# Linear attention and a gated feed-forward on one core: the second tile's loads ahead of the output weights, its attention inside the first tile's units, the first tile's outputs inside the second tile

## The chip, the cores and the metric

The kernel runs on one core of a Trainium2 chip. The metric is device time in microseconds, the median of the runs. One more execution was taken with the hardware profiler; every row shown comes from it. The engines are TensorE (PE in the profile; PEld is its weight load), VectorE (DVE), ScalarE (ACT), GpSimd (POOL) and SyncE (SP). Each works through its own instructions in the order in which they were issued, and waits at the first whose inputs or whose output buffer are not free.

## The reference

Decayed linear attention over 4 batches, 8 heads, 768 positions and 64 channels, in blocks, and then a gated feed-forward on the 3072 positions of width 512, with an inner width of 1536.

```python
for b in range(nb):                                # blocks of 64 positions
    intra = np.einsum('bhic,bhjc->bhij', qb, kb) * Dmask[None]
    intra = np.einsum('bhij,bhjd->bhid', intra, vb)
    inter = np.einsum('bhid,bhde->bhie', qb * lam_pow[None], kv_state)
    out[:, :, sl] = intra + inter
    kv_state = lam_block * kv_state + np.einsum('bhsd,bhse->bhde', kb * rev_pow[None], vb)
x = attn_out.transpose(0, 2, 1, 3).reshape(B * S, H * D)
g = x @ w_gate
out = (g * (1.0 / (1.0 + np.exp(-g))) * (x @ w_val)) @ w_out
```

## The kernel before, in words

The 768 positions are cut into six tiles (`NBLK`) of 128 positions; a tile holds all 4 batches, so 512 rows. For each tile the attention of the four batches gives `xt` (the feed-forward's input, transposed), then twelve `ffn_fc` units give the hidden rows, then four `ffn_out` give the output rows of the four batches.

The order is written by hand. Each tile has a list of units, and `pieces` says which parts of the attention are issued behind which unit: dictionaries `late` (tile 0), `second` (tile 1) and the result of `spread` (later tiles). The instructions of every engine stand in exactly this order.

A unit `ffn_fc` (L369) is four matmuls for `gp`, Silu on ScalarE, four matmuls for `vp`, and a product `h_sb` on VectorE. `gp` and `vp` take turns in three PSUM buffers (`gpsum`). An output `ffn_out` (L384) is twelve matmuls, a copy on ScalarE and a store from SP.

The attention of one batch of one tile has these parts. `prep_k` (L206) transposes K with eight matmuls, and ScalarE copies the result to `ktb` in two halves. `prep_q` (L214) transposes Q with four matmuls, and VectorE scales it into `qt`. `front` (L247) makes the scores, which VectorE masks into `ssb`; in tiles 0 and 1 it fills two score buffers, in later tiles one. `values` (L271) applies the scores to V and the state to Q; the result is copied to `xt`. `scale_v` (L298) makes the product `v_s` of V and the decay, in two halves of 64 partitions: on VectorE for tiles 0 and 1, on GpSimd from tile 2 on (`HALF`). `update` (L314) multiplies K by that product and brings the running state `kv` and its decayed form `kvd` up to date on VectorE; `cast_kv` copies the state to `kvb` on ScalarE. From tile 2 on, `update_mid` (L334), `cast_mid` and `update_end` do this in two steps of 64 positions. All PSUM tiles of the attention and of the outputs share three buffers (`apsum`), the scores have two (`spsum`).

In tile 2 (Q only) and from tile 3 on (`TURNED`; K and Q) the transposes are done by DMA instead, issued from SP (`turn`, L230).

Loads of K, Q, V and of the weights are issued from GpSimd, and they cast to bf16 on the way. They use eight semaphores in turn, so a load waits until the one eight before it has landed. K and V have three slots in SBUF; each needs its off-diagonal parts zeroed once, which GpSimd does with memsets for the slots 1 and 2. GpSimd issues, after the eight loads of the gate and value weights:

```python
nc.gpsimd.dma_start(out=wo_sb, in_=moe_w_out.rearrange("(c p) m -> p c m", p=128))
nc.gpsimd.memset(kvb[:, 0].bitcast(U32), 0)
zero_off(nc.gpsimd, ktb[:, 1])
for slot in (1, 2):
    for t in (kbd, vbd):
        zero_off(nc.gpsimd, t[:, slot])
load_k(1); load_qv(1, 2)
load_k(2); load_qv(2)
```

Tile 0 has the twelve units and then its own outputs (three whole, the last in two halves of the columns). The whole attention of tile 1 stands between these outputs. Tile 1 has only its twelve units, with the attention of tile 2 and the last two updates of tile 1 in between. From tile 2 on, the outputs of the tile before stand behind every third unit. The last tile's outputs end the kernel.

Of the kernel before, what the change touches and what calls it, by code (L numbers as in the profile page):

```python
# [21 lines left out]
def kernel(  # L22
# [73 lines left out]
    def load_k(tt):
        for c in range(2):
            load_bd(k, kbd, tt, c)

    def load_qv(tt, step=B, between=()):  # L100
        qn[tt] = load.tile([128, B, H, D], BF16, name="q_nat", tag="q_nat")
        for b in range(0, B, step):
            load_q(tt, b, b + step)
            for f, *on in between:
                f(*on)
            for c in range(2):
                load_bd(v, vbd, tt, c, b, b + step)
# [84 lines left out]
    wo_sb = const.tile([128, FC, DM], BF16, name="wo_sb")  # L192
# [13 lines left out]
    def prep_k(tt, b, pool=apsum, tag="a"):  # L206
        tk = pool.tile([128, 2, HP, 64], FP32, name="tk", tag=tag)
        for hp in range(HP):
            for c in range(2):
                nc.tensor.matmul(tk[:, c, hp, :], kbd[:, tt % SLOTS, c, b * HP + hp, :], eye2, start=True, stop=True)  # L210
        for h, ps in enumerate(HALVES):
            nc.scalar.copy(out=ktb[ps, tt % 2, :, b * HP:(b + 1) * HP, 64 * h:64 * h + 64], in_=tk[ps])  # L212
# [84 lines left out]

    def scale_v(tt, b):  # L298

        v_s = att.tile([128, HP, 2, D], BF16, name="v_s", tag="v_h" if tt >= HALF else "v_s")  # L300
        for h, ps in enumerate(HALVES):
            vb = vbd[ps, tt % SLOTS, 0, b * HP, 64 * h:64 * h + 64]
            eng = nc.gpsimd if tt >= HALF else nc.vector
            n = 1 if tt == NBLK - 1 else 2
            pv = bap(pw[ps], [[7, HP], [0, n], [0, D]], extra_offset=3) if tt >= HALF else \
                bap(pw[ps], [[7, HP], [1, n], [0, D]], extra_offset=2)
            eng.tensor_tensor(out=v_s[ps, :, 0:n], in0=bap(vb, [[128, HP], [128 * NP, n], [1, D]]), in1=pv,  # L307
                              op=ALU.mult)
        scaled[tt, b] = v_s
# [88 lines left out]
    for b in range(2):  # L398
        prep_q(0, b)
# [23 lines left out]
    load_qv(2)

    late = {1: []}
    for b in range(B):
        late.setdefault(3 * b, []).append((scale_v, 0, b))
        late[3 * b + 2] = [(update, 0, b)]  # L430
        late[3 * b + 3] = [(cast_kv, b)]
    late[1].append((zero_mid,))
    late[13] = [(prep, 1, 0, gpsum, "g"), (prep, 1, 1, gpsum, "g"), (scale_v, 1, 0)]
    late[14] = [(front, 1, 0), (front, 1, 1), (prep, 1, 2, gpsum, "g"), (prep, 1, 3, gpsum, "g"),
                (scale_v, 1, 1), (values, 1, 0)]
    late[15] = [(values, 1, 1), (front, 1, 2), (front, 1, 3), (update, 1, 0), (values, 1, 2),
                (update, 1, 1), (values, 1, 3), (cast_kv, 0), (cast_kv, 1)]

    def spread(tt, at, slots):

        for b, (s0, s1, s2, s3, s4) in enumerate(slots):
            for i, f, *on in ((s0, scale_q if tt >= TURNED else prep_k, tt, b), (s1, update_mid, tt, b),
                              (s2, cast_mid, b), (s2, front, tt, b), (s2, update_end, tt, b), (s3, values, tt, b),
                              (s4, cast_kv, b)):
                if f is not cast_kv or tt + 1 < NBLK:
                    at.setdefault(i, []).append((f, *on))
                if f is prep_k:
                    at[i].append((scale_q, tt, b))
        return at


    late[14].append((turn, 2, 2))
    late[15].append((scale_v, 1, 2))
    second = {0: [(update, 1, 2), (scale_v, 1, 3)], 1: [(cast_kv, 2)], 2: [(update, 1, 3)], 3: [(cast_kv, 3)]}
    second = spread(2, second, ((1, 2, 3, 4, 5), (3, 4, 5, 6, 7), (6, 7, 8, 9, 10), (7, 8, 9, 10, 11)))

    for tt in range(NBLK):
        units = [(ffn_fc, tt, fc) for fc in range(FC)]
        pieces = {}
        if tt == 0:  # L460
            units += [(ffn_out, 0, b) for b in range(3)] + [(ffn_out, 0, 3, i, 2) for i in range(2)]
            pieces = late
        else:
            if tt + 1 < NBLK:
                for b in range(2):
                    scale_v(tt + 1, b)
            rest = [(scale_v, tt + 1, b) for b in range(2, B)] if tt + 1 < NBLK else []
            if tt + 2 < NBLK:
                load_k(tt + 2)
                load_qv(tt + 2, between=rest)  # L470
            else:
                for f, *on in rest:
                    f(*on)
            if tt > 1:
                units = sum([units[3 * b:3 * b + 3] + [(ffn_out, tt - 1, b)] for b in range(B)], [])
            if tt == 1:
                pieces = second
            elif tt + 1 < NBLK:
                pieces = spread(tt + 1, {}, [(max(i - 1, 0), i, i + 1, i + 2, i + 3) for i in (0, 4, 8, 12)])
# [41 lines left out]
```

## Time and profile before

| | us |
|---|---|
| median of 3 runs (237.81 to 238.08) | 238.0 |
| the profiled execution | 239.77 |
| its span, first to last instruction | 238.0 |
| TensorE busy | 219.2 |
| VectorE busy | 122.7 |
| ScalarE busy | 123.4 |
| GpSimd busy | 102.5 |

The granted clock of TensorE is 1.00 throughout. The profiled execution's time contains 1.8 us around its span. These points in time help to read the timelines (us from the start of the span): first unit of tile 0 at 19.09; first output of tile 0 at 40.77; first unit of tile 1 at 59.04; first unit of tile 2 at 87.11; last matmul issued at about 234.

The loads, with the time from issue to landing: the last piece of the value weights issued at 17.20 lands 14.5 us later; the output weights issued at 17.93 land 21.5 us later; tile 1's K is issued from 29.74 and lands after 10.4 to 10.6 us; its last V is issued at 45.3 and lands after 4.8 us.

### The profile page before, as it was taken

What the parts mean: (1) busy time and instruction counts of PE and PEld (TensorE: products, weight loads), DVE (VectorE), ACT (ScalarE), POOL (GpSimd) and SP (SyncE); (2) the same over time, 40 slices, a digit from 0 to 9 for tenths busy, and PEclk for the clock granted to TensorE, in tenths of its full rate; (3) what the DMA queues carried; (4) which work ended last, traced back from release to release, by engine and by line L of the source; (5) the groups of instructions that cost most, each with busy time, mean ns of one, the idle gap of its engine ahead of it and who ended that gap; (6) DMA issues with size and microseconds to landing.
All of it is one profiled execution on the core that took longest, in us unless ns stands there. A gap on an engine that the chain in (4) does not pass through costs nothing.

```text
span 238.0 us, 4373 instructions
## 1 busy us (share of the span) xinstructions
PE 219.2 (92%) x1692; PEld 118.2 (50%) x1720; DVE 122.7 (52%) x233; ACT 123.4 (52%) x234; POOL 102.5 (43%) x125
## 2 busy tenths in 40 slices
PE   0598999988989997999999999999999999999994
PEld 0484454567455544455545545555455544444443
DVE  7685677288798677356457247336334412322100
ACT  7875644466758883546545545554534532232122
POOL 7999992891699319971997302200000000000000
PEclk9999999999999999999999999999999999999999
DMA  7999999999989994999999895100110110111022
GB/s 110 194 176 201 206 207 170 178 179 168 165 57 134 129 171 59 113 215 174 168 131 141 132 116 130 47 31 13 47 44 0 47 44 2 42 47 44 35 101 88
DMA packets 105269, 26.50 MB, mean 111 GB/s; under 512 B 96288, under 2 KB 102432, under 8 KB 105248
## 3 DMA queue, kind: packets, MB, share of 16 engines
q0 software_dynamic: 76400, 13.64, 74.9%
q1 hardware_dynamic: 28704, 12.59, 24.2%
q8 instruction: 13, 0.21, 0.3%
q14 instruction: 8, 0.07, 0.1%
q10 hardware_dynamic: 144, 0.00, 0.0%
HBM read 28.32 MB, written 6.29 MB: 145 GB/s over the span
## 4 chain that ended last, share of the span: by engine, by line
PE 60%; POOL 21%; DMA 15%; issue 2%; ACT 0%; POOLq 0%; ACTq 0%
PE ffn_op L391 22%; PE vp L381 17%; PE gp L376 17%; DMA vbd<-in_v_dram 10%; POOL kbd L86 5%; DMA q_nat<-in_q_dram 5%; POOL v_s L307 4%; POOL vbd L86 2%; POOL q_nat L92 1%; PE op L279 1%; PE sp L254 1%; PE op L280 1%; PE up L340 1%; POOL wv_sb L195 1%; POOL wg_sb L195 1%
## 5 line engine op out<-in xcount | busy, mean ns | idle before, releaser
L382 DVE TENSOR_TENSOR h_sb<-sil,vp 128x512 bf16<-128x512 bf16 x72 | 49.4, 686 | 85.5 <-PE vp L381 51.8
L381 PE MATMUL vp<-xt,wv_sb 128*128 128x512 bf16 x281 | 73.4, 379 | 0.5
L376 PE MATMUL gp<-xt,wg_sb 128*128 128x512 bf16 x274 | 72.0, 379 | 1.2 <-ACT xt L291 0.5
L378 ACT ACTIVATE sil<-gp 128x512 bf16<-128x512 f32 x72 | 43.0, 597 | 44.9 <-PE gp L376 40.8
L391 PE MATMUL ffn_op<-wo_sb,h_sb 128*128 128x512 bf16 (+1 forms) x305 | 64.3, 362 | 0.3
L307 POOL TENSOR_TENSOR v_s<-vbd,pw 64x512 bf16<-64x512 bf16 (+1 forms) x32 | 30.9, 966 | 43.5 <-DMA vbd<-in_v_dram 24.2
L381 PEld LDWEIGHTS <-wv_sb 128*128 128x128 bf16 x288 | 28.2, 98 | 34.0
L391 PEld LDWEIGHTS <-h_sb 128*128 128x128 bf16 x312 | 29.5, 98 | 28.6
L394 ACT COPY osb<-ffn_op 128x512 f32<-128x512 f32 (+1 forms) x26 | 14.4, 553 | 48.1 <-PE ffn_op L391 46.9
L376 PEld LDWEIGHTS <-wg_sb 128*128 128x128 bf16 x288 | 25.6, 98 | 25.4 <-issue 0.7
L86 POOL DMA_DIRECT2D vbd<-in_v_dram x32 | 24.3, 787 | 5.1 <-DMA wo_sb<-in_moe_w_out_dram 4.2
L86 POOL DMA_DIRECT2D kbd<-in_k_dram x24 | 19.9, 850 | 0.8 <-POOLq L505 0.8
L294 ACT CAST xt<-op 128x512 bf16<-128x512 f32 x23 | 13.5, 586 | 12.7 <-PE op L280 9.0
L332 ACT CAST kvb<-kv 64x256 bf16<-64x256 f32 x40 | 16.1, 403 | 0.7
L212 ACT CAST ktb<-tk 64x512 bf16<-64x512 f32 x24 | 13.9, 580 | 2.4 <-PE tk L210 2.1
L348 ACT CAST kvb<-mid 64x256 bf16<-64x256 f32 x32 | 12.9, 403 | 0.9 <-DVE mid L343 0.3
L307 DVE TENSOR_TENSOR v_s<-vbd,pw 64x512 bf16<-64x512 bf16 x16 | 12.5, 781 | 0.2
L256 DVE TENSOR_TENSOR ssb<-sp,mask 128x512 bf16<-128x512 f32 x16 | 10.9, 683 | 0.0
L217 PE MATMUL tq<-identity,q_nat 128*128 128x128 bf16 x32 | 4.0, 262 | 6.8 <-POOL identity masks.py:199 6.2
L267 DVE TENSOR_TENSOR ssb<-sp,mask 128x384 bf16<-128x384 f32 x16 | 8.1, 551 | 3.7 <-PE sp L265 3.7
L279 PE MATMUL op<-qt,kvb 128*128 128x64 bf16 x128 | 9.9, 193 | 0.1
L279 PEld LDWEIGHTS <-kvb 128*128 128x128 bf16 x128 | 8.7, 98 | 2.2 <-issue 0.3
(78 smaller groups left out, 187.7 us busy)
## 6 DMA issues: line engine op xcount, KB each, us to landing
out_dram<-osb SPq DMA_DIRECT2D x22, 256.0 KB, 2.0
kbd<-in_k_dram POOLq DMA_DIRECT2D x24, 128.0 KB, 5.0
q_nat<-in_q_dram POOLq DMA_DIRECT2D x4, 512.0 KB, 9.2
vbd<-in_v_dram POOLq DMA_DIRECT2D x16, 128.0 KB, 7.9
wo_sb<-in_moe_w_out_dram POOLq DMA_DIRECT2D x1, 1536.0 KB, 21.5
q_raw<-in_q_dram SPq DMA_DIRECT2D x4, 256.0 KB, 5.3
vbd<-in_v_dram POOLq DMA_DIRECT2D x16, 64.0 KB, 5.2
wg_sb<-in_moe_w_gate_dram POOLq DMA_DIRECT2D x2, 512.0 KB, 10.9
```

The lines of the kernel that those rows point to most:

```text
L86: nc.gpsimd.dma_start(out=dst[ps, tt % SLOTS, c, b0 * HP:b1 * HP, 64 * h:64 * h + 64], in_=bass.AP(tensor=t.tensor, offset=t.offset + ((b0 ...
L212: nc.scalar.copy(out=ktb[ps, tt % 2, :, b * HP:(b + 1) * HP, 64 * h:64 * h + 64], in_=tk[ps])
L279: nc.tensor.matmul(op[:, hp, cs], kvb[:, c, b, hp, :], qt[:, hp, cs], start=True, stop=False)
L294: nc.scalar.copy(out=xt, in_=op)
L307: eng.tensor_tensor(out=v_s[ps, :, 0:n], in0=bap(vb, [[128, HP], [128 * NP, n], [1, D]]), in1=pv, op=ALU.mult)
L332: nc.scalar.copy(out=kvb[ps, 0, b, :, 64 * h:64 * h + 64], in_=kvn[b][ps])
L376: nc.tensor.matmul(gp, wg_sb[:, mc, fs], xt[:, mc, :], start=(mc == 0), stop=(mc == MC - 1))
L378: nc.scalar.activation(sil, gp, AF.Silu)
L381: nc.tensor.matmul(vp, wv_sb[:, mc, fs], xt[:, mc, :], start=(mc == 0), stop=(mc == MC - 1))
L382: nc.vector.tensor_tensor(out=hs[tt][:, fc, :], in0=sil, in1=vp, op=ALU.mult)
L391: nc.tensor.matmul(op, hs[tt][:, fc, b * BLK:(b + 1) * BLK], wo_sb[:, fc, cs], start=(fc == 0), stop=(fc == FC - 1))
L394: nc.scalar.copy(out=osb, in_=op)
```

## The change

It has four parts, all in the order of work:

1. GpSimd zeroes slot 1 and loads all of tile 1 (K and Q by halves of the batches, then V by halves) before it issues the load of `w_out`; then it zeroes slot 2 and loads tile 2.
2. Tile 0 has only its twelve units. Its own updates stand behind every second unit. The K and Q transposes and scores of tile 1 stand behind units 8 to 11, and its values behind unit 11; the last `xt` is copied half by ScalarE, half by VectorE.
3. Tile 1 has sixteen entries: behind every third unit stands an output of tile 0. Tile 1's four `scale_v` and updates are in its entries 0 to 6, tile 2's attention in entries 6 to 15. Entries are numbered from 0, so 3, 7, 11 and 15 are the outputs.
4. Tile 2's Q is transposed on TensorE (`prep_q`) and no longer by DMA. The products `scale_v` of tile 2's batches 0 and 1 are made by VectorE; GpSimd makes those of batches 2 and 3 behind the loads of tile 3. From then on a tile's loads are in the order V, K, Q, and the places of the later tiles' pieces move by one or two entries.

```diff
-    nc.gpsimd.dma_start(out=wo_sb, in_=moe_w_out.rearrange("(c p) m -> p c m", p=128))
     nc.gpsimd.memset(kvb[:, 0].bitcast(U32), 0)
     zero_off(nc.gpsimd, ktb[:, 1])
-    for slot in (1, 2):
-        for t in (kbd, vbd):
-            zero_off(nc.gpsimd, t[:, slot])
-    load_k(1)
-    load_qv(1, 2)
-    load_k(2)
-    load_qv(2)
+    for t in (kbd, vbd):
+        zero_off(nc.gpsimd, t[:, 1])
+    for order in ((k, q), (v,)):
+        for b in (0, 2):
+            load_tile(1, order, b, b + 2)
+    nc.gpsimd.dma_start(out=wo_sb, in_=moe_w_out.rearrange("(c p) m -> p c m", p=128))
+    for t in (kbd, vbd):
+        zero_off(nc.gpsimd, t[:, 2])
+    load_tile(2, (k, q, v))
...
-        v_s = att.tile([128, HP, 2, D], BF16, name="v_s", tag="v_h" if tt >= HALF else "v_s")
+        v_s = att.tile([128, HP, 2, D], BF16, name="v_s", tag="v_h" if (tt, b) >= (HALF, 2) else "v_s")
...
-            eng = nc.gpsimd if tt >= HALF else nc.vector
+            eng = nc.gpsimd if (tt, b) >= (HALF, 2) else nc.vector
...
-    late = {1: []}
+    first = {}
     for b in range(B):
-        late.setdefault(3 * b, []).append((scale_v, 0, b))
-        late[3 * b + 2] = [(update, 0, b)]
-        late[3 * b + 3] = [(cast_kv, b)]
-    late[1].append((zero_mid,))
-    late[13] = [(prep, 1, 0, gpsum, "g"), (prep, 1, 1, gpsum, "g"), (scale_v, 1, 0)]
-    late[14] = [(front, 1, 0), (front, 1, 1), (prep, 1, 2, gpsum, "g"), (prep, 1, 3, gpsum, "g"),
-                (scale_v, 1, 1), (values, 1, 0)]
-    late[15] = [(values, 1, 1), (front, 1, 2), (front, 1, 3), (update, 1, 0), (values, 1, 2),
-                (update, 1, 1), (values, 1, 3), (cast_kv, 0), (cast_kv, 1)]
-    late[14].append((turn, 2, 2))
-    late[15].append((scale_v, 1, 2))
-    second = {0: [(update, 1, 2), (scale_v, 1, 3)], 1: [(cast_kv, 2)], 2: [(update, 1, 3)], 3: [(cast_kv, 3)]}
-    second = spread(2, second, ((1, 2, 3, 4, 5), (3, 4, 5, 6, 7), (6, 7, 8, 9, 10), (7, 8, 9, 10, 11)))
+        add(first, 2 * b, scale_v, 0, b)
+        add(first, 2 * b + 2, update, 0, b)
+        add(first, 2 * b + 3, cast_kv, b)
+    add(first, 1, zero_mid)
+    for i, f, b in ((8, prep_k, 0), (8, prep_q, 0), (9, prep_k, 1), (9, prep_q, 1), (9, front, 0), (10, front, 1),
+                    (10, prep_k, 2), (10, prep_q, 2), (10, prep_k, 3)):
+        add(first, i, f, 1, b)
+    first[11] = [(front, 1, 2), (prep_q, 1, 3, gpsum, "g"), (values, 1, 0), (front, 1, 3), (values, 1, 1),
+                 (values, 1, 2), (values, 1, 3, True)]
+    second = {}
+    for b, (s0, s1) in enumerate(((0, 2), (2, 3), (3, 5), (5, 6))):
+        add(second, s0, scale_v, 1, b)
+        add(second, s1, update, 1, b)
+        add(second, s1 + 1, cast_kv, b)
+    for b in range(2):
+        add(second, 7 + b, scale_v, 2, b)
+    spread(2, second, ((6, 8, 9, 10, 11), (7, 10, 11, 12, 13), (8, 11, 12, 13, 14), (9, 12, 13, 14, 15)))
...
         units = [(ffn_fc, tt, fc) for fc in range(FC)]
+        if tt:
+            units = sum([units[3 * b:3 * b + 3] + [(ffn_out, tt - 1, b)] for b in range(B)], [])
...
+            vs = [(tt + 1, b) for b in range(B) if (tt + 1, b) >= (HALF, 2)]
+            for on in vs[:-2]:
+                scale_v(*on)
             if tt + 2 < NBLK:
+                load_tile(tt + 2, (v, k, q))
+            for on in vs[-2:]:
+                scale_v(*on)
```

Here `add(at, i, piece...)` appends a piece behind entry `i`. The five numbers that `spread` takes for a batch are the entries of: transposes (K and Q); `update_mid`; `cast_mid`, `front` and `update_end`; `values`; `cast_kv`. `load_tile(tt, order, b0, b1)` issues the loads of the tensors in the order given, for the batches `b0` to `b1`.

More of the change, by code (lines that the diff above doesn't have):

```diff
@@ L94, in load_q, with load_tile @@
                                         ap=[[D, 128], [S * D, (b1 - b0) * H], [1, D]]))
[L96 to L107, printed above, removed]
+    def load_tile(tt, order, b0=0, b1=B):
+        for t in order:
+            if t is q:
+                if b0 == 0:
+                    qn[tt] = load.tile([128, B, H, D], BF16, name="q_nat", tag="q_nat")
+                load_q(tt, b0, b1)
+            else:
+                for c in range(2):
+                    load_bd(t, kbd if t is k else vbd, tt, c, b0, b1)
     q_raw = {}
@@ L212, in prep_k, with prep_q @@
             nc.scalar.copy(out=ktb[ps, tt % 2, :, b * HP:(b + 1) * HP, 64 * h:64 * h + 64], in_=tk[ps])
-    def prep_q(tt, b):
-        tq = apsum.tile([128, HP, 128], BF16, name="tq", tag="a")
+    def prep_q(tt, b, pool=apsum, tag="a"):
+        tq = pool.tile([128, HP, 128], BF16, name="tq", tag=tag)
         for hp in range(HP):
@@ L241, in scale_q @@
         scale(tt, qt, qt)
-    def prep(tt, b, *pool):
-        prep_k(tt, b, *pool)
-        prep_q(tt, b)
     def front(tt, b):
@@ L411 @@
     values(0, B - 1, split=True)
-    nc.gpsimd.dma_start(out=wo_sb, in_=moe_w_out.rearrange("(c p) m -> p c m", p=128))
     nc.gpsimd.memset(kvb[:, 0].bitcast(U32), 0)
     zero_off(nc.gpsimd, ktb[:, 1])
-    for slot in (1, 2):
-        for t in (kbd, vbd):
-            zero_off(nc.gpsimd, t[:, slot])
-    load_k(1)
-    load_qv(1, 2)
-    load_k(2)
-    load_qv(2)
-    late = {1: []}
-    for b in range(B):
-        late.setdefault(3 * b, []).append((scale_v, 0, b))
-        late[3 * b + 2] = [(update, 0, b)]
-        late[3 * b + 3] = [(cast_kv, b)]
@@ L439, in spread, with add @@
+    for order in ((k, q), (v,)):
[5 more added lines that the diff above has]
+    load_tile(2, (k, q, v))
+    def add(at, i, *piece):
+        at.setdefault(i, []).append(piece)
     def spread(tt, at, slots):
         for b, (s0, s1, s2, s3, s4) in enumerate(slots):
[L442 to L448, printed above, removed]
@@ L449, in spread @@
-        return at
-    late[14].append((turn, 2, 2))
-    late[15].append((scale_v, 1, 2))
-    second = {0: [(update, 1, 2), (scale_v, 1, 3)], 1: [(cast_kv, 2)], 2: [(update, 1, 3)], 3: [(cast_kv, 3)]}
-    second = spread(2, second, ((1, 2, 3, 4, 5), (3, 4, 5, 6, 7), (6, 7, 8, 9, 10), (7, 8, 9, 10, 11)))
+            if tt >= TURNED:
+                add(at, s0, scale_q, tt, b)
+            else:
+                add(at, s0, prep_k, tt, b)
+                add(at, s0, prep_q, tt, b)
+            add(at, s1, update_mid, tt, b)
@@ new lines, in spread @@
+            add(at, s2, cast_mid, b)
+            add(at, s2, front, tt, b)
+            add(at, s2, update_end, tt, b)
+            add(at, s3, values, tt, b)
+            if tt + 1 < NBLK:
+                add(at, s4, cast_kv, b)
+    first = {}
+    for b in range(B):
+        add(first, 2 * b, scale_v, 0, b)
[5 more added lines that the diff above has]
+        add(first, i, f, 1, b)
@@ L457 @@
     for tt in range(NBLK):
         units = [(ffn_fc, tt, fc) for fc in range(FC)]
+        if tt:
+            units = sum([units[3 * b:3 * b + 3] + [(ffn_out, tt - 1, b)] for b in range(B)], [])
         pieces = {}
[L460 to L467, printed above, removed]
-            if tt + 2 < NBLK:
[L469 to L479, printed above, removed]
+        if tt < 2:
+            pieces = (first, second)[tt]
+        elif tt + 1 < NBLK:
+            spread(tt + 1, pieces, [(i - 1, i, i + 1, i + 2, i + 3)
+                                    for i in ((2, 5, 9, 12) if tt == 2 else (1, 4, 8, 12))])
@@ L480 @@
+        if 0 < tt < NBLK - 1:
+            vs = [(tt + 1, b) for b in range(B) if (tt + 1, b) >= (HALF, 2)]
+            for on in vs[:-2]:
+                scale_v(*on)
+            if tt + 2 < NBLK:
+                load_tile(tt + 2, (v, k, q))
+            for on in vs[-2:]:
+                scale_v(*on)
         if tt and TURNED <= tt + 2 < NBLK:
-            for part, i in enumerate((4, 5, 6) if tt == 1 else (5, 6, 8)):
-                pieces.setdefault(i, []).append((turn, tt + 2, part))
+            for part, i in enumerate((9, 10, 12) if tt == 1 else (5, 6, 8)):
+                add(pieces, i, turn, tt + 2, part)
```

## The prediction

> **What bounds the kernel now.** I read the busy shares first, then who TensorE waited for, then the timelines of TensorE, VectorE, ScalarE and GpSimd from 16 to 92 us.
>
> ```profile
> PE 219.2 (92%) x1692; PEld 118.2 (50%) x1720; DVE 122.7 (52%) x233; ACT 123.4 (52%) x234; POOL 102.5 (43%) x125
> ```
>
> TensorE is the bound: it starts its feed-forward at 19.09 us and then hardly stops, so the change can only win what TensorE still waits for, less what it adds. Its list of waits (line waited for: us, times, longest):
>
> ```profile
> PE up L340 <- POOL v_s L307: 1.6, 1, 1.6
> PE up L320 <- DVE v_s L307: 1.1, 1, 1.1
> PE sp L263 <- DVE ssb L267: 1.0, 2, 0.5
> ```
>
> These end at 90.58, 65.92, 50.43 and 55.39 us. A matmul's row is longer than the step to the next one, so I count lost time from start to start. In the timeline of TensorE at the second tile's attention (start, duration, what, idle before):
>
> ```profile
> 49.70 0.22 PE L263 MATMUL sp<-qt,ktb 128*128 128x128 bf16 x1
> 49.76 0.19 PE L265 MATMUL sp<-qt,ktb 128*128 128x64 bf16 x1
> 50.43 0.22 PE L263 MATMUL sp<-qt,ktb 128*128 128x128 bf16 x1 [0.48 <-DVE ssb L267]
> ```
>
> The step behind a 128-column matmul is 0.056 us, behind a 64-column one 0.029; so the 0.48 costs 0.64. Counted so, the block from 45.7 to 59.0 loses 0.64+0.29+0.64+0.30+0.11 = 2.0 us. From 59.04 (tile 1's first unit) to 87.11 (tile 2's first) TensorE has 20.73 + 5.16 us of steps and takes 28.07: 2.2 lost, 1.2 of it before update(1,3). Then 1.7 before 90.58. In all 5.9 us; after that I find no real gap until the tail.
>
> VectorE's and GpSimd's timelines tell why 65.92 was late:
>
> ```profile
> 61.64 5.14 POOL L307 TENSOR_TENSOR v_s<-vbd,pw 64x512 bf16<-64x512 bf16 x4 [7.37 <-DMA vbd<-in_v_dram]
> 62.16 0.80 DVE L328 TENSOR_TENSOR kvd<-kv,pw 128x256 f32<-128x256 f32 x1
> 62.89 2.98 DVE L307 TENSOR_TENSOR v_s<-vbd,pw 64x512 bf16<-64x512 bf16 x2
> 65.90 0.69 DVE L382 TENSOR_TENSOR h_sb<-sil,vp 128x512 bf16<-128x512 bf16 x1
> ```
>
> One batch's product v_s takes VectorE 1.40 us elsewhere (21.72, 32.54), and 2.98 here, beside GpSimd's own products; h_sb, with one operand in PSUM, keeps its 0.69.
>
> **Steps used.** Unit (8 matmuls of 0.216) 1.73; output 2.59; update, K transposes, tile-2 scores .235 each; Q transposes .22; scores and values of tile 1 .34 and .56; values of tile 2 .47. VectorE, start to start: h_sb .60, product 1.40, kv .45, kvd .35, qt .41, ssb of tile 1 1.0, mid .41.
>
> **What is taken out.** The 2.0 us block goes (the outputs that stood in it move, 10.36 us unchanged; the two half-width outputs have the same columns). Of the 2.2 + 1.7, the causes go: update_mid(3,0) comes two units later and its product no longer stands behind a load queue late at 88. Minus 5.9.
>
> **Added on TensorE.** Tile 2's Q is transposed there, 16 x .056 = 0.9. The DMA transpose it replaces (turn, 59.10) was off the path; qt from PSUM costs VectorE .41 as it did from SBUF. The four stores move behind turn(3,0) and turn(3,1) on SP; SP is idle most of the time, three buffers cover, nothing. Four memsets move behind w_out on GpSimd: they delay only tile 2's loads.
>
> **Data.** The weights' last piece lands at 17.20+14.5 = 31.7. Tile 1's loads are now issued from 24.8 (17.93 and seven memsets of 0.98; before, 29.7), in halves of .70 and Q of 1.18 each, with one wait of 1.8 for the weights' landing, until 40.2; K and Q follow the weights at 1.6 to 1.7 us per half (the spacing of their landings at 40 to 46 before): K 33.4, Q 35.0, K 36.7, Q 38.3, against first use at 36.0 and 40.8. V lands by 39.5+4.8 = 44.3, used from 44.1 (first half, landed 41.5) and 47.5. w_out moved in 7.7 us once the weights were in (31.7 to 39.4); issued at 40.2 behind V it lands at 50 to 53, used at 54.7. All on time, margins of 1 to 4 us.
>
> **Last units of tile 0.** Updates now come every second unit. VectorE then has 2(.60)+1.40+.45+.35 = 3.4 us in 3.7; zero_mid (2.08 on ScalarE at 22.40) makes it late once, unit 5 waits .45 for h_sb of unit 3. Unit 11 ends at 19.09+20.73+.94+.45 plus 4 K, 3 Q, 2 scores (2.28) = 43.5. The new wait: ScalarE must copy ktb of batches 2 and 3 before unit 11's Silu. Before, the same four copies were:
>
> ```profile
> 46.63 2.37 ACT L212 CAST ktb<-tk 64x512 bf16<-64x512 f32 x4
> ```
>
> From 41.5: ktb 43.9, Silu 44.5, h_sb 45.15, ssb of batch 2 46.15, qt of batch 3 46.6. TensorE has scores 2, Q 3 and values 0 to do, until 44.6, and waits 2.0 for that qt before scores 3. Then values 1 to 3 (46.95 to 48.63) and, with no output to bridge it, the xt copy: .62, as at 18.47 to 19.09 before. Lost 0.45+2.0+0.62 = 3.1; tile 1's units begin at 49.25. Plus 3.1.
>
> **Tile 1.** VectorE now makes six products there (four of tile 1, two of tile 2 that were GpSimd's). Followed in queue order:
> - Output 0 ends at 57.25; product (1,1) is done at 57.5: .3.
> - Behind unit 4's h_sb (62.0) stand kv and kvd of batch 2 and product (1,3): 64.2. TensorE wants update(1,3) at 63.15: 1.15.
> - Output 1 takes a PSUM buffer that h_sb and kv (65.3) must free; TensorE is there at 65.0: .35.
> - Product (2,0) 66.3, qt, h_sb of unit 6 at 70.9, product (2,1), mid, qt of batch 2. Q transposes of batch 3 reuse that qt's PSUM buffer; TensorE is there at 73.0. With a product of 1.40 the qt is done at 73.1 (.2 with the hand-over), with 2.98 at 74.7 (1.85).
> - Output 2 waits for the next qt: .1 to .3.
>
> Which product holds depends on GpSimd: after w_out 41.3, memsets 45.1, tile 2's loads 53.5, tile 3's 8.3 us more, with waits for tile 2's landing (59 to 63): its own products start at 62 to 66.5 and eight halves, 4.4 to 5.1 per four, keep it until 71 to 76.7. Product (2,1), from 70.9, lies mostly inside. I take 1.85, for the 62.89 row is the same operation beside the same operation. Sum .3+1.15+.35+1.85+.1 = 3.75. Bounds: 2.2 with no overlap; 4.3 when product (1,3) is covered too.
>
> The Trainium skill ("SBUF — State Buffer", section "Who interferes with whom") speaks against this change: a VectorE instruction with two SBUF inputs and a GpSimd one that reads SBUF exclude each other, and the second blocks until the first ends. The rows agree (kvd and v_s slow down, h_sb doesn't). By that rule a product may wait for a whole GpSimd half on each of its halves, 2(.69+1.3) = 4.0 instead of 2.98, and the sum would be 1 us higher.
>
> Tiles 2 to 5 keep their steps; scale_q(3,0) needs the transposed Q at 94.5 and its queue entry is free at about 82 (6 to 10 us to land): nothing.
>
> **Sum.** -5.9 +0.9 +3.1 +3.75 = +1.85; I round the pieces down by 0.25, since the overlap covers not quite all of product (2,1): +1.6. The profiled execution took 239.77 us with a span of 238.0; the median of the runs is 238.0, and what lies around the span stays. So 239.6 us.
>
> **Rivals.**
> - *GpSimd's products miss VectorE's.* Tile 1 loses 2.2: +0.3, about 238.2, within 0.2% of before (about what a measurement can tell from no change). For: the start at 62 to 66.5 is uncertain and an early window ends at 71. Against: eight halves in a row are hard to miss. 0.19.
> - *VectorE keeps up*, the other side. Place: VectorE's queue between units 2 and 8 of tile 1. It decides at 1.9 us of waits in tile 1: below that the change wins. If h_sb, kv, kvd leave product (1,3) done by 63.5 and (2,1) is not covered, tile 1 loses 0.7 and the time is 236.8. For: over units 0 to 8 VectorE has 21.2 us of work in 23.7. Against: update(1,3) is wanted 1.8 us after unit 4's h_sb may start, with 2.8 us of work between. 0.22.
> - *w_out or V late.* Tile 2's K, issued from 45.1, shares the queues with w_out: +3.4 us (the spacing of a K) makes it 54 to 56.4, up to 1.7 lost on top: 241.2. 0.08.
> - *The data change does nothing*, TensorE still meets tile 1's K late. It would put 2 to 4 us at unit 8, 242 us; landing times speak against it: 0.03.
>
> **Chances.** Forecast 0.48. Faster by over 0.2%: 0.22. Same: 0.18, nearly all of the first rival. Slower: 0.60, the forecast, the late data and the edge of the first rival. The range, 237.0 to 241.0, runs from most of the second rival to the third.
>
> **To be seen in the profile of the changed kernel.** TensorE waiting about 2 us for qt before scores of batch 3, at 44 to 47 us; tile 1's first unit at 49 to 49.5; update(1,3) waiting over 1 us for v_s; VectorE's v_s of tile 2 with 2 to 3 us per product beside GpSimd's; tile 2's first unit at 90 to 91; no wait at its update_mid(3,0). A first unit of tile 1 before 48.5, or less than 1.9 us lost in tile 1, would make it wrong.

## The result, and the profile after

The changed kernel takes 242.31 us (median of four runs, 241.85 to 242.58) against 238.04 us (237.81 to 238.33) for the kernel before, a ratio of 1.0177 [1.0157, 1.0196]: 4.3 us slower, where 1.6 was forecast. The direction was right and the size wrong. The profiled execution took 242.42 us with a span of 240.6 us. In every run of this study the time is the span plus 1.8 us, so spans are compared with spans below and times with times.

The line of busy shares answers to the first one of the prediction:

```profile
PE 221.4 (92%) x1724; PEld 117.3 (49%) x1724; DVE 125.3 (52%) x238; ACT 123.2 (51%) x233; POOL 100.4 (42%) x125
```

TensorE has 2.2 us more of busy time, of which the 16 transposes explain some; it is still the bound. The rest has to stand in its waits (line waited for: us in all, times, longest):

```profile
PE sp L256 <- DVE qt L222: 2.0, 2, 1.7
PE tq L214 <- DVE qt L224: 2.0, 1, 2.0
...
PE up L313 <- DVE v_s L300: 1.0, 1, 1.0
...
PE op L273 <- DVE ssb L249: 0.4, 1, 0.4
```

Two of the three waits in the prediction's first list, those for GpSimd's v_s and for the masked scores ssb of tile 1, are gone. The third, of update(1,3) (tile 1, batch 3) for VectorE's v_s, is still there with 1.0 us; there its product is no longer slowed, but stands behind h_sb and the updates of batch 2. The others have come in their place. TensorE's timeline gives the places (start, duration, what, idle before):

```profile
46.26 0.22 PE L256 MATMUL sp<-qt,ktb 128*128 128x128 bf16 x1 [1.75 <-DVE qt L222]
...
64.03 0.39 PE L313 MATMUL up<-v_s,kbd 128*128 128x64 bf16 x8 [1.00 <-DVE v_s L300]
...
70.53 0.39 PE L207 MATMUL tk<-eye,kbd 128*128 128x64 bf16 x8 [0.28 <-ACT ktb L209]
...
75.32 0.38 PE L214 MATMUL tq<-identity,q_nat 128*128 128x128 bf16 x4 [1.98 <-DVE qt L224]
...
88.84 0.19 PE L273 MATMUL op<-ssb,vbd 128*128 128x64 bf16 x1 [0.41 <-DVE ssb L249]
```

The first is the wait at the end of tile 0, the second the one before update(1,3), the fourth the one for the PSUM buffer of Q of batch 2. The third and the last were not in the prediction. ScalarE's timeline has what two of the waits of tile 1 end with, the one before 70.53 and a short one of the values before 83.20:

```profile
69.31 1.17 ACT L209 CAST ktb<-tk 64x512 bf16<-64x512 f32 x2
...
82.33 0.82 ACT L341 CAST kvb<-mid 64x256 bf16<-64x256 f32 x2
```

Counted from start to start, as there, the end of tile 0 loses 0.21 (from 31.86 us), 1.92 (44.34) and 0.63 (the xt copy at 48.28), 2.76 us in all. Tile 1 loses 0.28 (56.94), 1.15 (62.88), 0.35 (64.73), 0.44 (70.09), 2.14 (73.18), 0.13 (77.97), 0.26 (82.94) and 0.57 (88.27), 5.32 us in all. Tile 1's first unit starts at 48.9 us, as forecast but for 0.1; tile 2's starts at 91.87, where 90 to 91 was forecast.

VectorE's timeline shows what holds the largest of them:

```profile
65.74 1.40 DVE L300 TENSOR_TENSOR v_s<-vbd,pw 64x512 bf16<-64x512 bf16 x2
...
71.74 2.74 DVE L300 TENSOR_TENSOR v_s<-vbd,pw 64x512 bf16<-64x512 bf16 x2
74.51 0.42 DVE L336 TENSOR_TENSOR mid<-kvd,up 128x256 f32<-128x256 f32 x1
74.85 0.42 DVE L224 TENSOR_TENSOR qt<-tq,qsc 128x512 bf16<-128x512 bf16 x1
...
85.00 1.07 DVE L353 TENSOR_TENSOR midd<-mid,pw 128x256 f32<-128x256 f32 x1
86.56 0.70 DVE L357 TENSOR_TENSOR kvd<-kv,pw 128x256 f32<-128x256 f32 x1
```

and GpSimd's timeline what lies beside it:

```profile
66.77 9.72 POOL L300 TENSOR_TENSOR v_s<-vbd,pw 64x512 bf16<-64x512 bf16 x8
...
84.75 4.51 POOL L300 TENSOR_TENSOR v_s<-vbd,pw 64x512 bf16<-64x512 bf16 x4
```

Product (2,0), at 65.74, is nearly over when GpSimd begins and takes the plain 1.40 us. Product (2,1), at 71.74, lies wholly inside GpSimd's eight halves and takes 2.74; behind it stand mid and the qt (74.85) for which TensorE waits until 75.32. GpSimd's next four halves, from 84.75 to 89.3, cover midd, which takes 1.07 us, and kvd 0.70; TensorE's values at 88.84 come late behind these. In the same stretches mid, kv and h_sb, each with one operand in PSUM, keep their 0.42, 0.42 and 0.68.

### The profile page after: what moved, and what is told of

The parts are those of the page before. It is cut to its first block, busy times and chain, and to the rows that moved or that the text cites. A ratio compares the mean times of both kernels' runs of the same rounds, so it can differ in the third digit from the quotient of the medians.

```text
span 240.6 us, 4415 instructions
## 1 busy us (share of the span) xinstructions
PE 221.4 (92%) x1724; PEld 117.3 (49%) x1724; DVE 125.3 (52%) x238; ACT 123.2 (51%) x233; POOL 100.4 (42%) x125
## 4 chain that ended last, share of the span: by engine, by line
PE 78%; DVE 10%; ACT 5%; DMA 2%; issue 2%; POOL 1%; DVEq 0%; ACTq 0%; POOLq 0%
PE ffn_op L384 25%; PE gp L369 22%; PE vp L374 22%; DVE v_s L300 3%; DVE h_sb L375 3%; DMA kbd<-in_k_dram 2%; ACT ktb L209 2%; PE op L273 2%; PE op L272 2%; DVE ssb L260 1%; PE sp L247 1%; PE sp L256 1%; POOL kbd L86 1%; PE up L333 1%; ACT sil L371 1%
## 5 line engine op out<-in xcount | busy, mean ns | idle before, releaser
L369 PE MATMUL gp<-xt,wg_sb 128*128 128x512 bf16 x288 | 74.0, 379 | 1.0 <-ACT xt L284 0.9
L384 PE MATMUL ffn_op<-wo_sb,h_sb 128*128 128x512 bf16 (+1 forms) x300 | 65.5, 370 | 0.2 <-DVE kv L317 0.2
L300 POOL TENSOR_TENSOR v_s<-vbd,pw 64x512 bf16<-64x512 bf16 (+1 forms) x28 | 26.8, 958 | 46.4 <-PE up L333 36.7
L384 PEld LDWEIGHTS <-h_sb 128*128 128x128 bf16 x300 | 28.4, 98 | 29.7 <-issue 0.3
L86 POOL DMA_DIRECT2D kbd<-in_k_dram x28 | 22.1, 817 | 3.1 <-DMA wv_sb<-in_moe_w_val_dram 1.7
L287 ACT CAST xt<-op 128x512 bf16<-128x512 f32 x22 | 12.9, 586 | 9.5 <-PE op L273 5.4
L300 DVE TENSOR_TENSOR v_s<-vbd,pw 64x512 bf16<-64x512 bf16 x20 | 15.0, 750 | 0.3
L214 PE MATMUL tq<-identity,q_nat 128*128 128x128 bf16 x48 | 5.5, 248 | 8.7 <-POOL identity masks.py:199 6.3
L273 PE MATMUL op<-ssb,vbd 128*128 128x64 bf16 x128 | 9.8, 193 | 0.4 <-DVE ssb L249 0.4
## 6 DMA issues: line engine op xcount, KB each, us to landing
wo_sb<-in_moe_w_out_dram POOLq DMA_DIRECT2D x1, 1536.0 KB, 13.4
```

The lines of the kernel that those rows point to most:

```text
L273: nc.tensor.matmul(op[:, hp, cs], vbd[:, tt % SLOTS, c, b * HP + hp, :], ssb[:, c, hp, :], start=False, stop=True)
L369: nc.tensor.matmul(gp, wg_sb[:, mc, fs], xt[:, mc, :], start=(mc == 0), stop=(mc == MC - 1))
L384: nc.tensor.matmul(op, hs[tt][:, fc, b * BLK:(b + 1) * BLK], wo_sb[:, fc, cs], start=(fc == 0), stop=(fc == FC - 1))
```

## The experiments

The theory to be tested had five parts. The loss is made of waits, each of them held by one engine's queue: 1.9 at the end of tile 0 (VectorE's and ScalarE's queue), 1.5 before update(1,3) (VectorE's), 2.6 for the PSUM buffers of the K and Q transposes (VectorE beside GpSimd), 0.8 further on (the same). The fifth part concerns the kernel before: some of its 5.9 us of gaps belonged to the one execution that was profiled. The rivals were that a wait taken away comes back at the next queue, and that the moved outputs or the data order cost time in themselves. The changed kernel's 242.31 us is from one set of runs. Beside the experiments the kernel before was run again, with medians from 238.14 to 238.49 us, so differences of 0.4 us between times of different sets tell little.

**The kernel before, profiled again.** No edit.

> The kernel of before, unchanged, profiled a second time. The first profiled execution took 239.77 us where the median of the runs is 238.0, and the change cost 4.3 us by the medians but 2.6 us by the spans of the two profiles (240.6 against 238.0). Theory 'the profile of before was a late one': most executions lose 1.7 us less than that profile, and most likely in its 1.74 us wait for GpSimd's product at 90.58 us, which hung on a DMA landing; then this span is 236.1 to 236.5 and that wait is 0 to 0.3 us. Rival 'the profile was typical and the rest is outside the span': span 238.0 again, the wait at 90.6 is again 1.5 to 1.9 us.

Measured: 238.49 us, ratio 1.0007 [0.9978, 1.0035], span 236.7 us where the first profile had 238.0. The lines of TensorE at update_mid(3,0), and of GpSimd's product that it waits for, are

```profile
89.33 0.39 PE L340 MATMUL up<-v_s,kbd 128*128 128x64 bf16 x8 [0.18 <-POOL v_s L307]
```

```profile
87.11 4.47 POOL L307 TENSOR_TENSOR v_s<-vbd,pw 64x512 bf16<-64x512 bf16 x4 [7.09 <-DMA vbd<-in_v_dram]
```

The first profile had 90.58 and 1.58 us of idle there, and the product at 88.37 behind 8.86 us for V. V landed 1.3 us earlier this time, and the wait shrank from 1.74 to 0.34, counted from start to start. The block is as before, with 0.64, 0.30, 0.64, 0.29 and 0.11. Tile 1 takes 28.44 us, from 58.82 to 87.26, so it loses 2.55 where the first profile had 2.2: 0.87 before update(1,3) instead of 1.24, and more further on. The spans of the runs of the kernel before range from 235.7 to 238.4 us, so the prediction's profile was one of the late ones. This execution, close to the median, loses 4.9 us, not 5.9.

**The same wait, by moving the work that waits.** Tile 2's pieces of tile 3 come later, with nothing else changed:

```diff
-                pieces = spread(tt + 1, {}, [(max(i - 1, 0), i, i + 1, i + 2, i + 3) for i in (0, 4, 8, 12)])
+                pieces = spread(tt + 1, {}, [(max(i - 1, 0), i, i + 1, i + 2, i + 3)
+                                             for i in ((2, 5, 9, 12) if tt == 2 else (0, 4, 8, 12))])
```

> The kernel of before with only tile 2's pieces of tile 3 moved to entries 2, 5, 9, 12, so that TensorE wants GpSimd's product of tile 3 two units later. It prices the 1.74 us wait of the first profile. Theory 'that wait was mostly a late DMA landing of one execution': the time falls by 0.2 to 0.6 us only, as the second profile's 0.34. Rival 'the wait is usual': it falls by 1.2 to 1.7 us.

Measured: 237.89 us, 0.9989 [0.9974, 1.0004], span 236.0. TensorE's timeline shows update_mid(3,0) with no idle before it:

```profile
90.90 1.03 PE L381 MATMUL vp<-xt,wv_sb 128*128 128x512 bf16 x4
91.76 0.40 PE L340 MATMUL up<-v_s,kbd 128*128 128x64 bf16 x8
```

The wait is gone and the median moves by 0.3 us (238.22 to 237.89), which the interval does not tell from no change. At most 0.6 us could be won there. Tile 1, where nothing was altered, loses 1.8 us in this profile, so its waits too differ from execution to execution, by some 0.7 us.

**The block of tile 1's attention in the kernel before.** Its order alone is interleaved so that VectorE keeps up:

```diff
-    late[14] = [(front, 1, 0), (front, 1, 1), (prep, 1, 2, gpsum, "g"), (prep, 1, 3, gpsum, "g"),
-                (scale_v, 1, 1), (values, 1, 0)]
-    late[15] = [(values, 1, 1), (front, 1, 2), (front, 1, 3), (update, 1, 0), (values, 1, 2),
+    late[14] = [(front, 1, 0), (prep, 1, 2, gpsum, "g"), (prep, 1, 3, gpsum, "g"), (front, 1, 1),
+                (scale_v, 1, 1)]
+    late[15] = [(front, 1, 2), (values, 1, 0), (values, 1, 1), (front, 1, 3), (update, 1, 0), (values, 1, 2),
```

> The kernel of before with only the order inside tile 1's attention block altered: K and Q transposes or values stand between the scores of one batch and of the next. Theory 'the block of before lost 2.0 us only because two batches' scores stood behind each other with two score buffers': the four waits of 0.64, 0.30, 0.64 and 0.29 us go and the time falls by 1.5 to 1.9 us, to about 236.4. Rival 'the block is bound by VectorE's ssb in any order': the waits come back at values or scores of batch 3 and the time falls by under 0.5 us.

Measured: 238.09 us, 0.9992 [0.9965, 1.0019], span 236.3. The block's waits fell from 1.98 to 0.92 us, yet the time stayed. TensorE's and GpSimd's lines tell where the 1.1 us went:

```profile
88.92 0.39 PE L340 MATMUL up<-v_s,kbd 128*128 128x64 bf16 x8 [1.23 <-POOL v_s L307]
```

```profile
86.72 4.46 POOL L307 TENSOR_TENSOR v_s<-vbd,pw 64x512 bf16<-64x512 bf16 x4 [6.89 <-DMA vbd<-in_v_dram]
```

update_mid(3,0) begins at 88.92 here and at 89.33 in the profile above. TensorE arrived 1.45 us earlier (87.53 against 88.98) and waited 1.38 us, counted from start to start, where it had waited 0.34, because GpSimd's product stands behind V's landing, which the block does not move. My expectation fell: most of what was won upstream was given back at a wait that the data set.

**GpSimd's products out of the way, in the changed kernel.** In tile 2, the loads of tile 4 are issued before the products of tile 3; nothing else moves:

```diff
-            for on in vs[:-2]:
+            n = 0 if tt == 2 else len(vs) - 2
+            for on in vs[:n]:
...
-            for on in vs[-2:]:
+            for on in vs[n:]:
```

> The changed kernel with one part altered: in tile 2's stretch GpSimd issues the loads of tile 4 before its products of tile 3's batches 0 and 1, so that it makes no product between about 71.5 and 80 us. Theory 'VectorE's product of batch 1 of tile 2 is slowed by GpSimd's products': that product falls from 2.74 to 1.40 us, TensorE's wait for qt before the Q transposes of batch 3 from 2.14 to 0.6 to 0.9 us, and the time by 1.2 to 1.5 us, to about 240.9. Rival 'VectorE's queue alone holds TensorE up': the product is shorter but the wait moves behind it, and the time falls by under 0.5 us.

Measured: 240.99 us, 1.0097 [1.0064, 1.0129], span 239.2. VectorE's and GpSimd's lines:

```profile
71.75 1.40 DVE L300 TENSOR_TENSOR v_s<-vbd,pw 64x512 bf16<-64x512 bf16 x2
...
73.52 0.42 DVE L224 TENSOR_TENSOR qt<-tq,qsc 128x512 bf16<-128x512 bf16 x1
```

```profile
67.52 4.36 POOL L300 TENSOR_TENSOR v_s<-vbd,pw 64x512 bf16<-64x512 bf16 x4
...
71.83 3.30 POOL L86 DMA_DIRECT2D vbd<-in_v_dram  x4
```

GpSimd now ends its first four halves as product (2,1) begins, which takes 1.40 us instead of 2.74, at the same start. The wait behind it falls from 2.14 to 0.79, and the time by 1.3 us, as expected. The overlap of this one product is shown to cost 1.3 us.

**VectorE's two products of tile 2 left out.** In their place tile 1's products are used again:

```diff
+        if tt == 1:
+            kept[b] = v_s
...
+    def reuse(b):
+        scaled[2, b] = kept[b]
...
-        add(second, 7 + b, scale_v, 2, b)
+        add(second, 7 + b, reuse, b)
```

> The changed kernel with VectorE's products of tile 2's batches 0 and 1 left out: the updates of these two batches multiply tile 1's products once more, so TensorE's work and all waits but these two products stay. Theory 'the two products that moved to VectorE cost what is lost at 70 to 75 us': the waits of 0.44 and 2.14 us there fall to 0.2 to 0.4 us together, those of 1.15 and 0.35 us at 63 and 65, which stand before these products in the queue, stay, and the time falls by 2.0 to 2.4 us, to about 240.1. Rival 'VectorE is late in tile 1 by its whole load': the waits before them shrink as well, by 1 us or more.

Measured: 240.34 us, 1.0092 [1.0073, 1.0112], span 238.5. The wait of 2.14 us is gone, the 0.44 has become 0.21 (at Q of batch 2, still behind ScalarE's ktb copies), a new one of 0.84 stands at 75.75, and those of 0.28, 1.16 and 0.35 stay. The two products cost 2.0 us where they stand; the other half of the loss does not come from them. The wait of 0.57 at 88.27 is gone too. TensorE and VectorE come to this place 1.5 us earlier here, and midd and kvd of batch 2 are done before GpSimd begins at 85.03:

```profile
83.50 0.41 DVE L360 TENSOR_TENSOR midd<-mid,pw 128x256 f32<-128x256 f32 x1
...
84.40 0.43 DVE L364 TENSOR_TENSOR kvd<-kv,pw 128x256 f32<-128x256 f32 x1
```

**The same two products given back to GpSimd.** This undoes one part of the change:

```diff
-        v_s = att.tile([128, HP, 2, D], BF16, name="v_s", tag="v_h" if (tt, b) >= (HALF, 2) else "v_s")
+        v_s = att.tile([128, HP, 2, D], BF16, name="v_s", tag="v_h" if (tt, b) >= (HALF, 0) else "v_s")
...
-            eng = nc.gpsimd if (tt, b) >= (HALF, 2) else nc.vector
+            eng = nc.gpsimd if (tt, b) >= (HALF, 0) else nc.vector
...
-    for b in range(2):
-        add(second, 7 + b, scale_v, 2, b)
...
-            vs = [(tt + 1, b) for b in range(B) if (tt + 1, b) >= (HALF, 2)]
+            vs = [(tt + 1, b) for b in range(B) if (tt + 1, b) >= (HALF, 0)]
```

> The changed kernel with one part undone: GpSimd makes the products of tile 2's batches 0 and 1 again, ahead of its loads of tile 3. Theory 'a product on VectorE and a product beside GpSimd's cost the same 1.4 us, whoever makes it': the 0.44 and 2.14 us at 70 to 75 go (as where they were left out), but GpSimd's products now run from about 60 to 65 us, over VectorE's product of tile 1's batch 3 at 62.6 us, which takes 2.7 to 3.0 us and makes the wait for update(1,3) 2.5 to 2.8 instead of 1.15; tile 3's loads come some 5 us later. The time falls by 0.5 to 1.2 us, to about 241.5. Rival 'the load of tile 3 behind them decides': TensorE waits at 75 to 95 us for tile 3's data or products, and the time rises.

Measured: 240.4 us, 1.0111 [1.0022, 1.0201], span 238.0. GpSimd and VectorE:

```profile
63.51 4.63 POOL L300 TENSOR_TENSOR v_s<-vbd,pw 64x512 bf16<-64x512 bf16 x4 [8.17 <-DMA vbd<-in_v_dram]
```

```profile
62.43 1.40 DVE L300 TENSOR_TENSOR v_s<-vbd,pw 64x512 bf16<-64x512 bf16 x2
...
64.91 1.22 DVE L321 TENSOR_TENSOR kvd<-kv,pw 128x256 f32<-128x256 f32 x1
```

GpSimd begins 1.1 us after product (1,3) does, too late to slow it (I had expected it slowed); it hits kvd, 0.42 us elsewhere, which takes 1.22. The median falls by 1.9 us, more than the 0.5 to 1.2 expected, since the wait of 2.14 goes and the 0.44 becomes 0.22. By the medians, undoing this one part gives back some 45% of the loss; the interval is wide, and reaches past the changed kernel's own ratio.

**Q of batch 3 transposed one unit earlier.**

```diff
-    first[11] = [(front, 1, 2), (prep_q, 1, 3, gpsum, "g"), (values, 1, 0), (front, 1, 3), (values, 1, 1),
+    add(first, 10, prep_q, 1, 3, gpsum, "g")
+    first[11] = [(front, 1, 2), (values, 1, 0), (front, 1, 3), (values, 1, 1),
```

> The changed kernel with one part altered: tile 1's Q transposes of batch 3 stand behind unit 10 instead of unit 11. Theory 'the 1.92 us wait at 44.3 us is VectorE's qt behind h_sb and ssb': qt of batch 3 is ready before unit 11 ends; what is next is the score buffer that ssb of batch 2 frees at about 45.4 us, so the wait falls to 0.9 to 1.2 us and the time by 0.8 to 1.0 us, to about 241.4. Rival 'ScalarE's copies set the end of the block whatever VectorE does': the xt copies move no earlier than by 0.3 us and the time stays within 0.3 us.

Measured: 241.7 us, 1.0146 [1.0092, 1.0201], span 239.9. TensorE's line before scores 3 now names another step:

```profile
45.30 0.22 PE L256 MATMUL sp<-qt,ktb 128*128 128x128 bf16 x1 [0.96 <-DVE ssb L260]
```

1.92 became 1.12 here and 0.29 after it, 0.5 us less. The median falls by 0.6, a little under the expected 0.8, with an interval that takes in no gain at all. The queue of copies on ScalarE ahead of unit 11's Silu is not moved by this edit.

**update(1,3) one entry later.** In the slots of tile 1 the last pair is (5, 7) instead of (5, 6), and product (2,0) goes to entry 6, product (2,1) to 8:

```diff
-    for b, (s0, s1) in enumerate(((0, 2), (2, 3), (3, 5), (5, 6))):
+    for b, (s0, s1) in enumerate(((0, 2), (2, 3), (3, 5), (5, 7))):
...
-        add(second, 7 + b, scale_v, 2, b)
+        add(second, (6, 8)[b], scale_v, 2, b)
```

> The changed kernel with one part altered: in tile 1 the update of batch 3 stands behind the output of entry 7 instead of unit entry 6, and VectorE's product of tile 2's batch 0 one entry earlier. Theory 'TensorE waits for VectorE's queue here, and an output in between covers it': the waits of 1.15 and 0.35 us at 62.9 and 64.7 go; VectorE's later products come earlier too, so the wait at 73 does not grow, and the time falls by 1.5 to 2.4 us, to about 240.3. Rival 'VectorE is simply full in tile 1': the 1.5 us come back as a longer wait at the Q transposes of batch 3, and the time falls by under 0.5 us.

Measured: 242.09 us, 1.0144 [1.0104, 1.0184], span 240.0. TensorE's timeline:

```profile
66.82 0.39 PE L207 MATMUL tk<-eye,kbd 128*128 128x64 bf16 x8 [0.44 <-ACT osb L387]
...
68.47 0.38 PE L214 MATMUL tq<-identity,q_nat 128*128 128x128 bf16 x4 [1.26 <-ACT ktb L209]
...
74.68 0.38 PE L214 MATMUL tq<-identity,q_nat 128*128 128x128 bf16 x4 [1.21 <-DVE qt L224]
```

The 1.15 and 0.35 us are gone, and 0.60 and 1.42 stand a few us later, on ScalarE's copies of an output (osb) and of K (ktb). The 0.44 is gone as well, and the 2.14 is 1.38: in this profile tile 1 loses 4.7 us instead of 5.3. By the medians 0.2 us is won. So the rival held for the waits that the edit was aimed at: their time comes back one queue on, though the holder is ScalarE, which the prediction had followed in tile 0 only.

**Tile 2's Q transposed by DMA again, as before the change.**

```diff
-                add(at, s0, prep_q, tt, b)
+                add(at, s0, scale_q, tt, b)
...
+    add(second, 4, turn, 2, 2)
```

> The changed kernel with one part undone: tile 2's Q is again transposed by DMA (issued behind entry 4 of tile 1) and scaled in place by VectorE. Theory 'the Q transposes on TensorE cost their 16 steps and, through the PSUM buffer that waits for VectorE's qt, most of the 2.14 us wait': 0.9 us of steps go, and the wait at 73 us goes or returns small at the scores or values behind (0.3 to 0.8 us): the time falls by 2.0 to 2.7 us, to about 239.9. Rival 'VectorE is behind anyway': the wait returns whole at the values of batch 0, and only the 0.9 us go.

Measured: 248.32 us, 1.0421 [1.0385, 1.0456], span 245.8. SP and VectorE:

```profile
59.63 5.40 SPq L234 DMA_TRANSPOSE qt<-q_nat  x1
```

```profile
72.50 0.47 DVE L224 TENSOR_TENSOR qt<-qt,qsc 128x512 bf16<-128x512 bf16 x1 [7.14 <-DMA qt<-q_nat]
72.89 2.98 DVE L300 TENSOR_TENSOR v_s<-vbd,pw 64x512 bf16<-64x512 bf16 x2
```

Both forecasts missed. The transpose, issued at 59.63, is used from 72.50; VectorE stands for it 7.14 us, then makes the slowed product, and TensorE waits 6.9 us for that. With the transpose issued at this place, sparing TensorE the 0.9 us costs 6; no other place was tried.

**The two repairs together** (the edits of the products and of Q of batch 3).

> The changed kernel with two of the single alterations together: Q transposes of batch 3 of tile 1 behind unit 10, and the loads of tile 4 ahead of GpSimd's products of tile 3. Theory 'the waits are separate': the gains add, 0.6 to 0.8 and 1.3 to 1.4 us, to about 240.2, still 0.8% slower than before. Rival 'the second wait is fixed by the time of the data': the earlier start of tile 1 is given back, and the time stays at 241.

Measured: 240.58 us, 1.0098 [1.0068, 1.0128], span 239.7. In the profile the waits of tile 0's end and tile 1 fall by 1.3 us, where the two repairs alone took 0.5 and 1.4 off them. By the medians 1.7 us is won, against 0.6 and 1.3, which cannot be told from a sum; by the ratios (1.0097 with the products alone) the second repair wins nothing. The profile shows why the gain is not whole. TensorE comes earlier against GpSimd, which waits for data until about the same time: product (2,1) begins at 71.64 and GpSimd runs from 67.88 to 72.25,

```profile
71.64 1.87 DVE L300 TENSOR_TENSOR v_s<-vbd,pw 64x512 bf16<-64x512 bf16 x2
```

so the product is partly covered again, and the wait is 1.27 us instead of 0.79. Even with both repairs the changed kernel is 1% slower than the one before.

**The kernel before, mended.** The first try took the interleaved block and the later pieces of tile 3 (both shown above), put update(1,3) one unit later, and some pieces of tile 2's batches 0 and 1 as well (not update_mid of batch 1, as the expectation has it, but its scores and what follows them):

```diff
-    second = {0: [(update, 1, 2), (scale_v, 1, 3)], 1: [(cast_kv, 2)], 2: [(update, 1, 3)], 3: [(cast_kv, 3)]}
-    second = spread(2, second, ((1, 2, 3, 4, 5), (3, 4, 5, 6, 7), (6, 7, 8, 9, 10), (7, 8, 9, 10, 11)))
+    second = {0: [(update, 1, 2), (scale_v, 1, 3)], 1: [(cast_kv, 2)], 3: [(update, 1, 3)], 4: [(cast_kv, 3)]}
+    second = spread(2, second, ((1, 2, 3, 5, 6), (3, 4, 6, 7, 8), (6, 7, 8, 9, 10), (7, 8, 9, 10, 11)))
```

> The kernel of before with the interleaved block and three more places: the update of batch 3 of tile 1 behind unit 3 instead of 2, values of tile 2's batch 0 and update_mid of its batch 1 one unit later, tile 2's pieces of tile 3 at entries 2, 5, 9, 12. Theory 'what the change was to win can be had without moving outputs or loads': of the second profile's waits the 2.0 us of the block, 0.87 at 64.5, 0.55 and 0.41 at 70 and 71 and 0.34 at 89 go, together 4.1; the time falls by 3.0 to 4.0 us, to 234.4 to 235.4. Rival 'VectorE is late in tile 1 here too': the waits in tile 1 come back behind the moved pieces and only the block's 1.5 to 1.9 us are won.

Measured: 237.15 us, 0.9946 [0.9926, 0.9967], span 235.8: 1.1 to 1.3 us won. TensorE has a new wait of 2.02 us, start to start, for an h_sb that stands behind a product covered by GpSimd's:

```profile
65.86 0.81 PE L376 MATMUL gp<-xt,wg_sb 128*128 128x512 bf16 x3 [1.87 <-DVE h_sb L382]
```

```profile
62.11 2.98 DVE L307 TENSOR_TENSOR v_s<-vbd,pw 64x512 bf16<-64x512 bf16 x2
```

The second try leaves update(1,3) where it was, and instead makes tile 1's products of batches 1 and 3 one place earlier, before GpSimd begins:

```diff
-    late[13] = [(prep, 1, 0, gpsum, "g"), (prep, 1, 1, gpsum, "g"), (scale_v, 1, 0)]
+    late[13] = [(prep, 1, 0, gpsum, "g"), (prep, 1, 1, gpsum, "g"), (scale_v, 1, 0), (scale_v, 1, 1)]
...
-    late[15].append((scale_v, 1, 2))
-    second = {0: [(update, 1, 2), (scale_v, 1, 3)], 1: [(cast_kv, 2)], 2: [(update, 1, 3)], 3: [(cast_kv, 3)]}
+    late[15] += [(scale_v, 1, 2), (scale_v, 1, 3)]
+    second = {0: [(update, 1, 2)], 1: [(cast_kv, 2)], 2: [(update, 1, 3)], 3: [(cast_kv, 3)]}
```

> The kernel of before with the interleaved block, the products of tile 1's batches 1 and 3 one place earlier (so that VectorE makes them before GpSimd's products begin at 61.6 us and before they stand ahead of ssb of batch 2), and tile 2's pieces of tile 3 at entries 2, 5, 9, 12. Theory 'the waits of before hang on VectorE's products standing beside GpSimd's or ahead of ssb': against the second profile of before 1.98 falls to 0.3 to 0.5, 0.87 to 0 to 0.2, 0.34 goes, 0.55 and 0.41 stay or halve; the time falls by 2.5 to 3.2 us, to about 235.4. Rival 'the waits only move', as in e7: at most 1.2 us.

Measured: 236.88 us, 0.9938 [0.992, 0.9957], span 234.8, which beats both kernels. All VectorE's products of tile 1 now lie before GpSimd's:

```profile
57.17 2.83 DVE L307 TENSOR_TENSOR v_s<-vbd,pw 64x512 bf16<-64x512 bf16 x4
```

```profile
61.34 4.41 POOL L307 TENSOR_TENSOR v_s<-vbd,pw 64x512 bf16<-64x512 bf16 x4 [6.58 <-DMA vbd<-in_v_dram]
```

Two products take 2.83 us, so 1.4 each. The waits that are left (0.12, 0.29 and 0.41 in the block; 0.31, 0.14, 0.56, 0.41, 0.12 and 0.35 in tile 1) make 2.7 us, 2.2 less than in the second profile of the kernel before. The spans of the two differ by 1.9 (236.7 to 234.8), since tile 0's first unit began 0.28 us later here (19.15 against 18.87). The medians differ by 1.6, against 2.5 to 3.2 expected. Three things were altered together, so the run does not price the moved products alone.

## Why the prediction was right in direction and wrong in size

Two terms of the sum failed, and both made the forecast too small: tile 1's waits, 3.75 for 5.32, and what is taken out, 5.9 for 4.9.

**What is taken out (5.9): read from a late execution.** The block's 2.0 us and the wait before 90.58 did go; update(1,3) kept 1.15 us, as the prediction's own list for tile 1 has it. But the wait before 90.58 was 1.74 in the profile that the prediction read and is 0.34 in the next, and removing it alone moves the median by 0.3. In all the second profile loses 4.9 us. That is 1.0 of the miss of 2.7. The prediction then put the sum, made on the execution of 239.77 us, on the median of 238.0. It had the two numbers side by side, and read the span of 238.0 as though it agreed with a time of 238.0. On its own scale the sum gives 241.4, nearer to the 242.42 of the changed kernel's profile.

**End of tile 0 (3.1): right, 0.3 too much.** The wait for qt before scores 3 was 1.92 (2.0 forecast), the xt copy 0.63 (0.62), h_sb 0.21 (0.45, and before unit 7, not 5, counted from 0). ScalarE's four copies stand at 41.23 ahead of the Silu at 43.62, as foreseen:

```profile
41.23 2.37 ACT L209 CAST ktb<-tk 64x512 bf16<-64x512 f32 x4 [0.46 <-PE tk L207]
43.62 0.60 ACT L371 ACTIVATE sil<-gp 128x512 bf16<-128x512 f32 x1
```

**Tile 1 (3.75): the larger failure; mechanism right, the term too small, 5.32 measured.** The five waits of the list came where they were placed, with 0.28, 1.15, 0.35, 2.14 and 0.13 for 0.3, 1.15, 0.35, 1.85 and 0.1. Three more, which the prediction put at nothing, come to 1.27 together. Two of them end with ScalarE, a queue that I had followed in tile 0 and not in tile 1. The 0.44 at 70.09 ends with the ktb copies; it halves when VectorE's two products are elsewhere, though the copies stand as they did, and why the transposes of K need not wait then was not found out. The 0.26 at 82.94 ends with the copies of mid to kvb, which stand behind an output's copy from 80.89 and two of kv; mid itself was done by 79.0, and GpSimd makes no product there. The 0.57 at 88.27 comes from VectorE's short chain of state updates, slowed beside GpSimd's products at 84.75 to 89.3: midd and kvd take 0.9 us more than alone. The prediction priced the overlap for the products alone. The run without VectorE's two products, where midd and kvd fall ahead of GpSimd's, does not have this wait; no run took the state updates out by themselves.

**Rounding down by 0.25** was the wrong way: product (2,1) was covered throughout, and its wait came out larger than the sum had it.

**Added on TensorE (0.9), the stores, the memsets, the data: as forecast.** w_out landed 13.4 us after its issue at 39.47, at 52.9, and TensorE waited for none of the loads of tile 1 or w_out. The rival on late data fell with that, and so did the one that the data change does nothing.

**The sum with what was measured:** -4.9 + 0.9 + 2.76 + 5.32 = +4.1, against +4.3 between the medians and +3.9 between the profiled spans (236.7 and 240.6). The miss of 2.7 is 1.0 (taken out) - 0.3 (end of tile 0) + 1.6 (tile 1) + 0.25 (rounding); that is 2.5, and 0.2 is left open. It was made after the fact, with the waits of one execution of each kernel. It leaves little for the rival that the moved outputs or the data order cost time in themselves, which no run tested alone.

**The two rivals of faster and same** hung on whether GpSimd's products miss VectorE's. They ran from 66.77 to 76.4, a little after the latest start forecast (66.5) and to the forecast end, and hit one product of the two. Had both missed, the run with the loads ahead tells the time: 240.99, still slower, as the rest of the loss does not hang on it.

**The rule on shared ports** ("SBUF — State Buffer", "Who interferes with whom", in the Trainium skill) spoke against this change, and the traces agree with its direction: one product of VectorE alone takes 1.40 us, beside GpSimd's 1.87, 2.74 or 2.98, while h_sb, with one operand in PSUM, keeps its 0.69. The estimate made from it for a fully covered product, 4.0 us, was not reached in any run.

## What to carry to other kernels

Compare a profile's span with spans and its time with times, and before a wait on a load is counted as a gain, see in a second execution whether it is there. Following the in-order queues, instruction by instruction, foretold each large wait here to 0.3 us; the waits missed were on the queue that was not followed to the end (ScalarE) and on small operations beside GpSimd that were not priced. What was won upstream of a wait that a landing set was mostly given back there, until that wait was moved too. And work of VectorE with both operands in SBUF did better before GpSimd's than beside it (1.40 us a product against up to 2.98), as the best kernel here has it.

## What was not expected of the hardware

- When V landed varied from execution to execution of one kernel: GpSimd's product of tile 3 began at 88.37, 87.11 and 86.72 us in three profiles where the work before it on GpSimd is the same (the third with another order of the block on the other engines), and the spans of the kernel before range over 2.7 us (235.7 to 238.4).
- The DMA transpose issued at 59.63 us, while GpSimd's loads were on their way, landed 12.8 us later; for 7.1 us of that VectorE stood waiting for it. In the kernel before, the same transpose, issued at 59.10, landed after 6.7 us.
- Short operations can lose more by the overlap than their own length: kvd went from 0.42 to 1.22 us, midd from 0.41 to 1.07.
